# First three pairs' scores through four PSUM banks in place of two, with six entries of the emission table moved

## Chip, cores and metric

One NeuronCore of a Trainium2 chip runs the whole program. The metric is device microseconds (us) of one execution; the kernel before was timed three times, and a fourth execution was profiled.

## What is computed

Causal attention with a decay bias over 4 batches, 8 heads, 576 tokens and 64 channels a head; then a network with a spatial mix over the tokens, then one with a token shift. The numpy reference, cut:

```python
scores = (1/8) * q @ k.T
cum = cumsum(log(clip(f, 1e-4, 1)))
scores = where(causal, -1e9, scores + cum[:, None] - cum[None, :])
attn = exp(scores - max(scores)); attn = attn / (sum(attn) + 1e-9)
x = (attn @ v).transpose(0, 2, 1, 3).reshape(4, 576, 512)

h = relu(x @ w_in); u, v = h[..., :512], h[..., 512:]
x = (u * (w_spatial @ layernorm(v) + b_spatial)) @ w_out

xs = x shifted by one token
xk = mu_k * x + (1 - mu_k) * xs; xr = mu_r * x + (1 - mu_r) * xs
out = sigmoid(xr @ w_r) * (relu(xk @ w_k) ** 2 @ w_v)
```

## The kernel before

The 32 heads are worked in 16 pairs, p = 0 to 15, four to a batch. Most products keep fp32 accuracy by splitting an operand into two fp16 halves, high and low, and multiplying the halves.

A pair goes through these steps. Lines are in brackets.

- **Preparation.** ACT takes sums of squares of k and q (`qksq`, L70). PE totals them (L77), and DVE makes a power-of-two scale (L84, L85, L87, L243, L91). The high half of k is made on POOL (L254) from pair 1 on, that of q on DVE (L258); the low halves, nk and nq, on DVE (`qklo`, L266). SP then transposes each by DMA into kT and qT (L268). Copies of their halves go into kA (`kaux`, L274, L275) and qA (`qaux`, L280), with the decay rows.
- **Scores.** `score` (L298) writes, for each of two heads, four units u of one PSUM bank each: 512 columns; 448 and 64; 320 and 192; 64. Each column block is the sum of a kT by qT product and a kA by qA product. `rowmax` (L309, DVE) adds the mask, copies a unit into sx and keeps the row's maximum in nm. That frees the bank.
- **Row sums.** POOL makes nb from nm (L318), and ACT takes exponentials of sx with their sums (L321). `mrow` takes the logarithm on ACT (L330), splits the result into three halves on DVE (L331 to L335), transposes on PE (L337), copies to mr on DVE (L339) and sends three rows into qA by SP (L341).
- **Second scores.** `scoreT` (L352, PE) makes the transposed scores with those rows, ACT their exponentials e (L362, L358), POOL sets the causal zeros (L366, L360).
- **Products.** PE multiplies e by v (L393), ACT and DVE write the two halves of xt (L396, L400), and the first network starts on them: m1v (L530), m1u (L598), m2 (L615).

Beside the first pairs run the loads and the splitting of the first network's weight w_in, block by block: load into wst (L96), ACT L103, DVE L106, L110 and L111, ACT L70 for a sum of squares, then L446 on ACT and L447 on DVE.

PSUM is four pools of two banks: `psm` (tag m: an offset matmul at the start, then the first networks), `pss` (tag s: the scores), `pst` (tag t: second scores) and `pso` (products, totals and small transposes). The first networks also take banks of `pss` and `pst` later on.

The order comes from times. Each step is added with a planned time and a priority; the plan is run in order of time, and a scheduler that keeps the program's dependencies then sets each engine's order. Table P (L33) holds the offsets, in units of half a pair. `L1` to `L3` shift the whole preparation of pairs 1 to 3, by

```python
A = T - P[f"L{p}"]
```

so that a smaller entry makes it later. `wd` is the spacing of the w_in blocks, and `vl1`, `vl2` are the times at which v of batches 1 and 2 is loaded. In program text, tiles are rotated by three: qT_133, qA_134, kT_131 and kA_132 belong to pairs 1, 4, 7 and so on, qT_137, qA_138, kT_135 and kA_136 to pairs 2, 5, 8, and qT_129, qA_130, kT_127 and kA_128 to pairs 0, 3, 6. nm_159 serves even pairs, nm_160 odd ones.

Of the kernel before, what the change touches and what calls it, by code (L numbers as in the profile page):

```python
# [7 lines left out]
F32 = mybir.dt.float32  # L8
# [17 lines left out]
T3 = ((0, 0), (0, 1), (1, 0))  # L26
# [3 lines left out]
SU = (((4, 0, 512, 0),), ((3, 0, 448, 0), (4, 512, 64, 448)), ((2, 0, 320, 0), (1, 0, 192, 320)), ((0, 0, 64, 0),))  # L30


P = dict(load=-8.0, sq=-5.52, ss=-5.2, sc=-5.0, hik=-5.196, lok=-4.166, hiq=-4.2, loq=-3.95, aux=-3.539, s=-2.53, m=-0.78, t=0.0, tu=0.426, th=0.412, pv0=0.2, pv1=0.9, out=1.405, rc=1.219, nr=1.831, xs=0.977, xl=1.55, rs=0.06, w1=-3.8, w0=2.0, s1=1.5, s0=6.8, wd=0.6, sd=0.6, wsp=9.493, eb=13.318, ed=1.1, crow=-4.2, mlp0=2.7, mlp1=2.7, mlp2=3.608, mlp3=2.7, len0=6.684, len1=6.952, len2=6.757, len3=4.319, T1=0.0, T2=0.0, T3=0.02, T4=0.0, T5=0.0, T6=0.0, T7=0.044, L1=0.0, L2=-0.017, L3=0.0, L4=0.0, L5=-0.224, L6=-0.408, L7=0.04, v0=-3.174, vs0=0.15, T8=0.0, T9=0.0, T10=0.0, T11=0.0, T12=-0.061, T13=-0.031, T14=0.069, T15=0.0, L0=0.0, L8=0.0, L9=0.0, L10=0.0, L11=0.0, L12=0.0, L13=-0.003, L14=0.0, L15=-0.24, vl1=-5.062, vq1=-2.7, vl2=-4.971, vq2=-2.898, vl3=-3.679, vq3=-3.376, lv0=0.238, lu0=0.381, lg0=0.249, lv1=0.238, lu1=0.381, lg1=0.199, lv2=0.238, lu2=0.381, lg2=0.436, lv3=0.346, lu3=0.381, lg3=0.701, n1=0.385, n2=0.508, n3=1.019, n4=1.161, gs=0.05, ta=3.45, tb=1.65, tc=0.22, fnb=1, fnk=1, fvn=1, fwf=0, fwin=0, fwsp=0)  # L33

# [7 lines left out]
class K:  # L44
# [201 lines left out]
    def qkhi(self, p, nm, eng):  # L246
# [5 lines left out]
        if eng == "act":  # L252
            if P["fnk"] > 0.5 and p >= 1:
                self.nc.gpsimd.tensor_scalar(hi, src, s, None, op0=ALU.mult)  # L254
# [37 lines left out]
    def score(self, g, u):  # L292

        p, h = divmod(g, 2)
        s = self.s[u % 2] = self.pss.tile([128, 512], F32, tag="s", name="s")
        for ib, k0, n, o in SU[u]:
            for j, (qn, kn, r) in enumerate((("qT", "kT", 128), ("qA", "kA", 67))):
                self.nc.tensor.matmul(s[:, o:o + n], self.tok(qn, p, h, 128 * ib - 64, 128)[0:r], self.tok(kn, p, h, k0, n)[0:r], start=(j == 0), stop=(j == 1))  # L298
# [13 lines left out]
    def rowsum(self, g, blocks):  # L312
# [4 lines left out]
        nb = self.at.tile([128, 10], F32, tag="nb", bufs=4, name="nb")  # L317
        (self.nc.gpsimd if P["fnb"] > 0.5 else self.nc.vector).tensor_scalar(nb[:, c], self.nm[p % 2][:, c], qa[:, 5:6], -1.0, op0=ALU.mult, op1=ALU.mult)  # L318
        for ib in blocks:
# [107 lines left out]
    def wconv(self, i):  # L427
# [3 lines left out]
        wf = self.wf[i] = self.stp.tile([128, 512], F32, tag="wf", bufs=4, name="wf")  # L431
        self.raw_convert(self.wst[i], wf, True, P["fwf"] > 0.5)
        self.sumsq(self.am[:, kc:kc + 1], wf, self.win[:, 0, kc, cs])
# [6 lines left out]
    def wsplit(self, i):  # L440
# [4 lines left out]
        hi, lo = self.win[:, 0, kc, cs], self.win[:, 1, kc, cs]  # L445
        self.pin(nc.gpsimd.tensor_scalar(hi, wf, s, None, op0=ALU.mult) if P["fwin"] > 0.5 else nc.scalar.mul(hi, wf, s))  # L446
        nc.vector.scalar_tensor_tensor(lo, wf, s, hi, ALU.mult, ALU.subtract)  # L447

    def weights_spatial(self):
# [31 lines left out]
        for c in range(5):  # L481
            if c < 4:
                hi, lo, r = self.wspT[:, 2 + c], self.wspT[:, 6 + c], slice(0, 128)
            else:
                hi, lo, r = self.wspT[:, 0], self.wspT[64:128, 1], slice(64, 128)
            self.pin(nc.gpsimd.tensor_scalar(hi, ws[:, c], s, None, op0=ALU.mult) if P["fwsp"] > 0.5 else nc.scalar.mul(hi, ws[:, c], s))
            self.pin(nc.vector.scalar_tensor_tensor(lo, ws[r, c], s[r], hi[r], ALU.mult, ALU.subtract))
# [81 lines left out]
    def ln3(self, b, j):  # L569
        nc, tn = self.nc, KB[j][1]  # L570
        v, mv = self.vv[j]
        cp = nc.gpsimd.tensor_copy if P["fvn"] > 0.5 else nc.scalar.copy
        nc.vector.tensor_scalar(v[:tn], v[:tn], mv[:tn, 0:1], mv[:tn, 2:3], op0=ALU.subtract, op1=ALU.mult)
# [570 lines left out]
```

## Time and profile before

| | |
|---|---|
| three timed runs | 688.99, 689.62, 691.65 us; median 689.62 |
| profiled execution | 684.6 us, its span 682.9 us |
| PE busy | 616.9 us, 90% of the span |
| ACT busy | 462.7 us, 68% |
| DVE busy | 436.3 us, 64% |
| POOL busy | 186.5 us, 27% |
| mean granted TensorE clock | 0.98 |

The span runs from the first to the last instruction of the profiled execution. An engine's share is an average over stages that differ: the attention of the first pairs, before the networks have work for PE, is where PE's share is smallest. A wait in the trace names the engine that waits, what it waits for, and the engine that ended the wait.

### The profile page before, as it was taken

The page shows a single profiled execution, that of the slowest core. Times are in us where ns is not written, and L with a number is a line of the kernel's source. Part 1 is how long each engine was busy: PE and PEld are TensorE (multiplying, and loading weights), DVE is VectorE, ACT ScalarE, POOL GpSimd, SP SyncE. Part 2 cuts the span into 40 slices and gives each one's busy share as a digit, 9 for nine tenths or more (in the row PEclk, how much of TensorE's full clock was granted, in tenths as well). Part 3 has the DMA queues.
Part 4 walks back from the last instruction along what each step waited for, and adds up shares of the span by engine and source line. Part 5 has one row for each costly group of instructions (what it writes and reads, how often), then busy time and mean ns, then how long its engine had stood idle before and what let it go on. Part 6 is the DMA issues. An engine that isn't in the chain of part 4 may idle for free.

```text
span 682.9 us, 11117 instructions
## 1 busy us (share of the span) xinstructions
PE 616.9 (90%) x3720; PEld 369.7 (54%) x3720; DVE 436.3 (64%) x1238; ACT 462.7 (68%) x1023; POOL 186.5 (27%) x420
## 2 busy tenths in 40 slices
PE   0478676998999999989999899999999999999997
PEld 0133333566545666446657544566655556566585
DVE  6885957879487867676137888997228524532342
ACT  4689899898879879788339599974328334442531
POOL 6342444674447743465106010000000000000000
PEclk9998898999999999999999999999999999999999
DMA  7984542627654555341046672313001100100010
GB/s 254 266 229 94 139 116 52 207 57 196 167 129 108 94 172 132 74 91 33 19 154 212 206 253 70 123 62 108 15 1 32 62 1 0 62 1 0 1 62 31
DMA packets 69343, 69.74 MB, mean 102 GB/s; under 512 B 46659, under 2 KB 47395, under 8 KB 69286
## 3 DMA queue, kind: packets, MB, share of 16 engines
q1 hardware_dynamic: 68854, 67.85, 35.5%
q10 hardware_dynamic: 432, 1.18, 0.4%
q8 instruction: 29, 0.48, 0.3%
q14 instruction: 28, 0.23, 0.1%
HBM read 43.61 MB, written 9.55 MB: 78 GB/s over the span
## 4 chain that ended last, share of the span: by engine, by line
PE 59%; DVE 14%; DMA 10%; ACT 7%; SPq 3%; issue 3%; POOL 2%; DVEq 0%; ACTq 0%
PE m L927 37%; PE o L393 4%; PE t L352 4%; DVE sx L309 4%; PE m L615 4%; PE s L298 3%; PE m1u L598 3%; DMA qA<-qT 3%; PE m1v L530 3%; SPq L341 2%; DMA qT<-nq 2%; ACT junk L70 2%; DMA wst<-in_moe_w_r_dram 2%; ACT junka L321 1%; DMA kT<-nk 1%
## 5 line engine op out<-in xcount | busy, mean ns | idle before, releaser
L321 ACT ACTIVATE junka<-sx,nb,qa 128x576 bf16<-128x576 f32 (+4 forms) x160 | 103.8, 648 | 20.5 <-POOL nb L318 17.3
L927 PE MATMUL m<-moe_w_v,k 128*128 128x512 f32 x432 | 111.6, 406 | 0.0
L927 PE MATMUL m<-xx,moe_w_k 128*128 128x512 f16 (+1 forms) x480 | 99.1, 358 | 0.6 <-ACT tmp L976 0.6
L927 PEld LDWEIGHTS m<-moe_w_v,k 128*128 128x128 f32 x432 | 80.7, 188 | 19.4
L309 DVE CUSTOM_DVE_ANT_0 sx<-s,mask 128x512 f32<-128x512 f32 (+4 forms) x160 | 72.5, 473 | 21.5 <-PE s L298 17.6
L298 PE MATMUL s<-kT,qT 128*128 128x512 f16 (+2 forms) x192 | 55.3, 308 | 25.3 <-DVE nm L309 14.2
L362 ACT ACTIVATE e<-t,qa 128x512 f32<-128x512 f32 x96 | 64.1, 680 | 18.5 <-PE t L352 18.0
L366 POOL TENSOR_SCALAR_AFFINE_SELECT e<-e 128x128 f32<-128x128 f32 x128 | 48.1, 388 | 85.2 <-ACT e L362 82.5
L927 PEld LDWEIGHTS <-moe_w_k 128*128 128x128 f16 x480 | 45.5, 98 | 47.6 <-issue 5.3
L976 ACT ACTIVATE tmp<-m,sx 128x512 f32<-128x512 f32 (+1 forms) x40 | 25.9, 647 | 58.6 <-PE m L927 58.6
L977 DVE TENSOR_TENSOR tmp<-tmp 128x512 f32<-128x512 f32 (+1 forms) x40 | 25.5, 638 | 56.9 <-ACT tmp L976 56.9
L393 PE MATMUL o<-e,v 128*64 128x64 f32 (+4 forms) x384 | 55.0, 410 | 5.2 <-DVE mr L339 1.9
L298 PE MATMUL s<-kA,qA 67*128 67x512 f16 (+2 forms) x192 | 49.0, 307 | 9.1 <-DMA qA<-qT 5.8
L899 POOL COPY x<-x 128x1 f32<-128x1 f32 x16 | 4.8, 313 | 185.5 <-ACT x L897 175.7
L615 PE MATMUL m<-wspT,vn 128*128 128x288 f16 x384 | 55.2, 286 | 0.2
L927 PE MATMUL m<-gh,moe_w_out 128*128 128x512 f16 (+1 forms) x240 | 50.9, 367 | 3.3 <-DVE gs L803 3.3
L352 PE MATMUL t<-qA,kA 70*128 70x512 f16 (+2 forms) x192 | 48.9, 292 | 3.9 <-DMA qA<-mr 2.9
L598 PE MATMUL m1u<-xt,win 128*128 128x288 f16 x384 | 52.3, 287 | 0.0
L352 PE MATMUL t<-qT,kT 128*128 128x512 f16 (+2 forms) x192 | 50.8, 292 | 0.0
L530 PE MATMUL m1v<-win,xt 128*128 128x512 f16 x192 | 49.4, 392 | 0.6 <-ACT xt L396 0.6
L927 PE MATMUL m<-moe_w_r,xx 128*128 128x512 f16 x216 | 48.0, 379 | 0.0
L949 DVE SCALAR_TENSOR_TENSOR mt<-x,mu,mt 128x64 f32<-128x64 f32 (+4 forms) x64 | 30.2, 514 | 26.7 <-ACT mt L947 26.7
(219 smaller groups left out, 1134.7 us busy)
## 6 DMA issues: line engine op xcount, KB each, us to landing
knat<-in_k_dram SPq DMA_DIRECT2D x16, 320.0 KB
v<-in_v_dram SPq DMA_DIRECT2D x20, 256.0 KB
gd<-u SPq DMA_DIRECT2D x16, 288.0 KB
gl<-gd SPq DMA_DIRECT2D x8, 576.0 KB
out_dram<-o SPq DMA_DIRECT2D x18, 256.0 KB
qnat<-in_q_dram SPq DMA_DIRECT2D x14, 320.0 KB
wst<-in_moe_w_k_dram SPq DMA_DIRECT2D x8, 512.0 KB
g<-gd SPq DMA_DIRECT2D x16, 256.0 KB
```

The lines of the kernel that those rows point to most:

```text
L298: self.nc.tensor.matmul(s[:, o:o + n], self.tok(qn, p, h, 128 * ib - 64, 128)[0:r], self.tok(kn, p, h, k0, n)[0:r], start=(j == 0), stop=( ...
L309: self.nc.vector.tensor_tensor_reduce(out=self.sx[g][r0:, SO[ib] + k0:SO[ib] + k0 + n], in0=self.s[u % 2][r0:, o:o + n], in1=self.mask[r0: ...
L321: self.nc.scalar.activation(self.junka[r, 0:n], self.sx[g][r, SO[ib]:SO[ib] + n], AF.Exp, scale=qa[r, 5:6], bias=nb[r, i:i + 1], accum_out ...
L352: self.nc.tensor.matmul(t[:, o:o + n], self.tok(kn, p, h, 128 * c, 128)[0:r], self.tok(qn, p, h, q0, n)[0:r], start=(j == 0), stop=(j == 1))
L362: self.nc.scalar.activation(self.e[g][:, 512 * u:512 * u + 512], t, AF.Exp, scale=self.qa[p][:, 5:6])
L366: self.nc.gpsimd.affine_select(out=e, in_=e, pattern=[[1, 128]], compare_op=ALU.is_ge, fill=0.0, base=0, channel_multiplier=-1)
L393: self.chain(self.nc.tensor.matmul(o[r, 448 + f:448 + q1], v[:, c, pr, r], e, start=(c == 0), stop=(c == 4 or q1 == 64)))
L530: nc.tensor.matmul(self.m1p, xt[:, xs, 128 * j:128 * j + 128], self.win[:, ws, kc, 512:1024], **flags)
L598: self.nc.tensor.matmul(o, self.win[:, ws, kc, fs], self.xt[(4 * b + kc) % 8][:, xs, ts_], start=(kc == 0 and n == 0), stop=(kc == 3 and n ...
L615: nc.tensor.matmul(o, pairs[n][0], pairs[n][1], start=(n == 0), stop=(n == 13))
L927: self.nc.tensor.matmul(out, l, r, start=(first and j == 0), stop=(last and j == len(pairs) - 1))
L949: nc.vector.scalar_tensor_tensor(tmp[:, r0:r1], x2[:, kc, r0:r1], self.mu[:, w, 1, kc:kc + 1], tmp[:, r0:r1], ALU.mult, ALU.add)
```

## The change

Score units with an odd u of pairs 0, 1 and 2 take their bank from `psm` in place of `pss`. Six entries of the table move. No instruction is added or removed; the wait each score unit needs for its bank goes to another bank.

```diff
 P = dict(
...
-wd=0.6
+wd=0.664
...
-L1=0.0, L2=-0.017, L3=0.0
+L1=-0.036, L2=-0.11, L3=-0.093
...
-vl1=-5.062
+vl1=-5.303
...
-vl2=-4.971
+vl2=-4.818
...
     def score(self, g, u):

         p, h = divmod(g, 2)
-        s = self.s[u % 2] = self.pss.tile([128, 512], F32, tag="s", name="s")
+        s = self.s[u % 2] = self.psm.tile([128, 512], F32, tag="m", name="s") if p < 3 and u % 2 else self.pss.tile([128, 512], F32, tag="s", name="s")
```

The scheduler answers with other orders on all engines, up to the row of PE that stands about 205 us into the profile of before; behind it they are the same. Three places follow.

On DVE, where pair 0's rowmax begins (sx, nm_159) and a w_in block is converted (wst, wf), the difference reads:

```order
-L106 TENSOR_SCALAR wst<-wst 128x512
 L258 TENSOR_SCALAR nq<-qnat_89,qa 128x10x64
 L266 SCALAR_TENSOR_TENSOR nq<-qnat_89,qa,nq 128x10x64
+L266 SCALAR_TENSOR_TENSOR nk<-knat_86,qa,nk 128x10x64
+L309 ISA sx,nm_159<-s,mask 128x512
+L309 ISA nm_159 128x1
+L106 TENSOR_SCALAR wst<-wst 128x512
+L309 ISA sx,nm_159<-s,mask 128x448
```

Pair 1's nk and pair 0's first rowmax now stand ahead of that block's conversion, and the second unit is read while the block is still being converted.

On DVE, a little later, where pair 2 is prepared (qnat_90) and pair 1's rowmaxes run (nm_160), the rows of the change that are new or kept read:

```order
+L84 TENSOR_SCALAR qa<-o 128x2
+L85 TENSOR_SCALAR qa<-qa 128x2
+L309 ISA sx,nm_160<-s,mask 128x512
+L309 ISA nm_160 128x1
+L87 TENSOR_SCALAR qa<-qa 128x2
+L309 ISA sx,nm_160<-s,mask 128x448
+L309 ISA nm_160 128x1
+L309 ISA sx,nm_160<-s,mask,nm_160 128x64
+L309 ISA nm_160 128x1
 L243 SCALAR_TENSOR_TENSOR qa<-qa 128x1
 L258 TENSOR_SCALAR nq<-qnat_90,qa 128x10x64
```

Before, L84, L85 and L87 stood together with L243 and L258 behind them, and the rowmaxes of pair 1 came after nq; now the first three rowmaxes of head 0 come between L85 and L243.

On SP, from pair 2's first transpose on:

```order
 L268 DMA_TRANSPOSE qT_137<-nq 128x10x128
+L214 DMA qnat_90<-in_q_dram 128x640
+L268 DMA_TRANSPOSE kT_135<-nk 128x10x128
+L280 DMA qA_138<-qT_137 64x1280
+L341 DMA qA_130<-mr 1x10x128 x3
+L274 DMA kA_136<-kT_135 64x1280
+L214 DMA knat_87<-in_k_dram 128x640
+L214 DMA qnat_88<-in_q_dram 128x640
+L214 DMA knat_85<-in_k_dram 128x640
+L268 DMA_TRANSPOSE kT_127<-nk 128x10x128
+L341 DMA qA_134<-mr 1x10x128 x3
+L268 DMA_TRANSPOSE qT_129<-nq 128x10x128
```

Pair 2's copy into qA (qA_138) now stands ahead of pair 0's mr rows (qA_130); before it stood behind them. Pair 3's kT transpose (kT_127) stands ahead of pair 1's mr rows (qA_134), and its qT transpose behind them; before, both stood behind.

Further on, DVE's L331 to L335 of pair 2 come ahead of pair 3's first rowmax, where they came behind it and among the others.

## Rows read from the trace of the kernel before

**Rows 1.** Busy time by stretches: start:end, its length, busy time (instructions), clock, DMA share.

```profile
17.00:31.00 14.00, 7.06 (x26) 2.91 (x25) 12.36 (x35) 7.94 (x21) 5.02 (x6) 1.00 0.95 265
31.00:60.00 29.00, 20.83 (x106) 10.85 (x106) 21.55 (x88) 25.70 (x64) 12.03 (x21) 0.99 0.58 164
60.00:83.00 23.00, 16.09 (x79) 7.35 (x79) 18.49 (x56) 18.90 (x45) 8.70 (x15) 0.72 0.72 162
83.00:117.00 34.00, 24.40 (x172) 12.86 (x169) 22.64 (x94) 33.03 (x80) 15.45 (x30) 0.95 0.30 76
117.00:683.00 566.00, 546.86 (x3336) 334.13 (x3334) 349.90 (x942) 369.45 (x801) 133.93 (x308) 0.99 0.31 89
```

The columns after the length are PE, PEld, DVE, ACT and POOL.

**Rows 2.** Waits of 17 to 58 and 60 to 117: total, times, longest.

```profile
DVE sx L309 <- PE s L298: 2.5, 6, 0.6
...
PE s L298 <- DVE nm L309: 6.1, 6, 2.2
...
PE s L298 <- DVE nm L309: 6.4, 7, 2.8
```

**Rows 3.** Timeline of PE: scores of pairs 1 and 2, second scores of 2 and 4.

```profile
34.38 0.96 PE L298 MATMUL s<-kA,qA 67*128 67x512 f16 x2 [2.35 <-DMA qA<-qT]
...
47.07 0.59 PE L298 MATMUL s<-kA,qA 67*128 67x512 f16 x1 [0.42 <-DMA qA<-qT]
...
84.72 0.38 PE L352 MATMUL t<-qA,kA 70*128 70x512 f16 x1
...
116.33 0.59 PE L352 MATMUL t<-qA,kA 70*128 70x512 f16 x1 [1.40 <-DMA qA<-mr]
```

**Rows 4.** Timeline of DVE around pair 0's rowmax: start, duration, engine, line, tiles, idle.

```profile
20.56 1.76 DVE L111 SCALAR_TENSOR_TENSOR wf<-wst,wf 128x512 int32<-128x512 int32 x1
22.24 0.87 DVE L266 SCALAR_TENSOR_TENSOR nk<-knat,qa,nk 128x640 f16<-128x640 f32 x1
23.04 0.68 DVE L309 CUSTOM_DVE_ANT_0 sx<-s,mask 128x512 f32<-128x512 f32 x1
...
30.14 0.23 DVE L309 CUSTOM_DVE_ANT_0 sx<-s,mask 64x64 f32<-64x64 f32 x1
```

**Rows 5.** Timeline of SP's DMA queue, pairs 1 and 2.

```profile
25.49 1.77 SPq L268 DMA_TRANSPOSE qT<-nq  x1
...
30.06 0.47 SPq L280 DMA_DIRECT2D qA<-qT  x1
...
34.82 2.84 SPq L268 DMA_TRANSPOSE qT<-nq  x1
...
41.21 2.39 SPq L341 DMA_DIRECT2D qA<-mr  x3
...
44.34 0.54 SPq L280 DMA_DIRECT2D qA<-qT  x1
```

**Rows 6.** Timeline of DVE, preparation of pair 2.

```profile
32.08 0.16 DVE L84 TENSOR_SCALAR qa<-o 128x2 f32<-128x2 f32 x1 [1.70 <-PE o L77]
...
33.91 0.89 DVE L266 SCALAR_TENSOR_TENSOR nq<-qnat,qa,nq 128x640 f16<-128x640 f32 x1
```

**Rows 7.** The page's group of all rowmaxes: count, busy time, mean ns, idle.

```profile
L309 DVE CUSTOM_DVE_ANT_0 sx<-s,mask 128x512 f32<-128x512 f32 (+4 forms) x160 | 72.5, 473 | 21.5 <-PE s L298 17.6
```

**Rows 8.** Timeline of DVE, pair 2's mr.

```profile
72.08 1.29 DVE L331 SCALAR_TENSOR_TENSOR ln<-ln,qa,nm 128x10 f32<-128x10 f32 x1
...
80.59 0.28 DVE L339 CAST mr<-o 30x128 f16<-30x128 f32 x1
```

**Rows 9.** Timeline of ACT: pair 2's logarithm and pair 3's first exponential.

```profile
70.09 0.30 ACT L330 ACTIVATE ln<-sa,tiny 128x10 f32<-128x10 f32 x1
...
74.86 0.87 ACT L321 ACTIVATE junka<-sx,nb,qa 128x576 bf16<-128x576 f32 x1 [3.02 <-POOL nb L318]
```

**Rows 10.** Timeline of PE behind 117 us: the same product twice.

```profile
117.99 1.91 PE L530 MATMUL m1v<-win,xt 128*128 128x512 f16 x4
...
122.25 1.02 PE L530 MATMUL m1v<-win,xt 128*128 128x512 f16 x4
```

More of the change, by code (lines that the diff above doesn't have):

```diff
@@ L30 @@
 SU = (((4, 0, 512, 0),), ((3, 0, 448, 0), (4, 512, 64, 448)), ((2, 0, 320, 0), (1, 0, 192, 320)), ((0, 0, 64, 0),))
-P = dict(load=-8.0, sq=-5.52, ss=-5.2, sc=-5.0, hik=-5.196, lok=-4.166, hiq=-4.2, loq=-3.95, aux=-3.539, s=-2.53, m=-0.78, t=0.0, tu=0.426, th=0.412, pv0=0.2, pv1=0.9, out=1.405, rc=1.219, nr=1.831, xs=0.977, xl=1.55, rs=0.06, w1=-3.8, w0=2.0, s1=1.5, s0=6.8, wd=0.6, sd=0.6, wsp=9.493, eb=13.318, ed=1.1, crow=-4.2, mlp0=2.7, mlp1=2.7, mlp2=3.608, mlp3=2.7, len0=6.684, len1=6.952, len2=6.757, len3=4.319, T1=0.0, T2=0.0, T3=0.02, T4=0.0, T5=0.0, T6=0.0, T7=0.044, L1=0.0, L2=-0.017, L3=0.0, L4=0.0, L5=-0.224, L6=-0.408, L7=0.04, v0=-3.174, vs0=0.15, T8=0.0, T9=0.0, T10=0.0, T11=0.0, T12=-0.061, T13=-0.031, T14=0.069, T15=0.0, L0=0.0, L8=0.0, L9=0.0, L10=0.0, L11=0.0, L12=0.0, L13=-0.003, L14=0.0, L15=-0.24, vl1=-5.062, vq1=-2.7, vl2=-4.971, vq2=-2.898, vl3=-3.679, vq3=-3.376, lv0=0.238, lu0=0.381, lg0=0.249, lv1=0.238, lu1=0.381, lg1=0.199, lv2=0.238, lu2=0.381, lg2=0.436, lv3=0.346, lu3=0.381, lg3=0.701, n1=0.385, n2=0.508, n3=1.019, n4=1.161, gs=0.05, ta=3.45, tb=1.65, tc=0.22, fnb=1, fnk=1, fvn=1, fwf=0, fwin=0, fwsp=0)
+P = dict(load=-8.0, sq=-5.52, ss=-5.2, sc=-5.0, hik=-5.196, lok=-4.166, hiq=-4.2, loq=-3.95, aux=-3.539, s=-2.53, m=-0.78, t=0.0, tu=0.426, th=0.412, pv0=0.2, pv1=0.9, out=1.405, rc=1.219, nr=1.831, xs=0.977, xl=1.55, rs=0.06, w1=-3.8, w0=2.0, s1=1.5, s0=6.8, wd=0.664, sd=0.6, wsp=9.493, eb=13.318, ed=1.1, crow=-4.2, mlp0=2.7, mlp1=2.7, mlp2=3.608, mlp3=2.7, len0=6.684, len1=6.952, len2=6.757, len3=4.319, T1=0.0, T2=0.0, T3=0.02, T4=0.0, T5=0.0, T6=0.0, T7=0.044, L1=-0.036, L2=-0.11, L3=-0.093, L4=0.0, L5=-0.224, L6=-0.408, L7=0.04, v0=-3.174, vs0=0.15, T8=0.0, T9=0.0, T10=0.0, T11=0.0, T12=-0.061, T13=-0.031, T14=0.069, T15=0.0, L0=0.0, L8=0.0, L9=0.0, L10=0.0, L11=0.0, L12=0.0, L13=-0.003, L14=0.0, L15=-0.24, vl1=-5.303, vq1=-2.7, vl2=-4.818, vq2=-2.898, vl3=-3.679, vq3=-3.376, lv0=0.238, lu0=0.381, lg0=0.249, lv1=0.238, lu1=0.381, lg1=0.199, lv2=0.238, lu2=0.381, lg2=0.436, lv3=0.346, lu3=0.381, lg3=0.701, n1=0.385, n2=0.508, n3=1.019, n4=1.161, gs=0.05, ta=3.45, tb=1.65, tc=0.22, fnb=1, fnk=1, fvn=1, fwf=0, fwin=0, fwsp=0)
 PRIO = 300
```

## The prediction

> **What bounds the kernel now.** I read the busy time by stretches first, then the waits, then the timelines around the first pairs. In the table by stretches [rows 1] look at PE against the length of each stretch: from 117 us to the end it works 546.86 of 566 us, so what is early or late there stays so to the end. Before 117 PE idles (6.9 of 14, 8.2 of 29, 6.9 of 23, 9.6 of 34 us) and another engine sets the pace: DVE in 17 to 31 (12.36 of 14, with the DMA engines at 0.95), ACT in 31 to 60 (25.70 of 29) and again in 83 to 117 (33.03 of 34). Between these ACT stretches, in 60 to 83, ACT has 4.1 us free. So a change among the first pairs is worth what it does to ACT's clock position at 83 and to PE's at 117, and no more.
>
> The waits [rows 2] show what four banks aim at: PE waits 6.1 us in 17 to 58 for a rowmax to free a bank, and 6.4 us in 60 to 117. Two readings limit this. The second sum belongs to pairs 3 to 5, whose scores keep two banks. And in 17 to 58 DVE, the other side of the exchange, waits only 2.5 us for PE: the rowmaxes, not the matmuls, are the longer half.
>
> **The banks.** Eight score units of each of the first three pairs now turn through four banks. PE writes all four before the first is free, so the most this can give is DVE's wait, 2.5 us over three pairs [rows 2], and the least is nothing. Pair 2's share of it (about half) falls after 47 us, where ACT is full, so I take 1.2 us, and only on DVE. The lenders lose nothing: the first networks' first matmul comes after these scores, since it needs pair 0's xt.
>
> The Trainium skill (Perfetto Trace Analysis, Matmuls) says that independent matmul groups should turn through different banks, so that the evacuation of one lies under the next one's matmuls; by that rule the 6.1 us of PE's wait would go. The rows on DVE disagree with taking that sum whole; what it would give is the second case below. Against the change speaks another page of the Trainium skill (TensorE: Matmul & The Clock Gate, A second HAM failure mode: psum-queue depth-cycling): cycling through banks left PE idle between groups often enough for its clock to go up and down. Here the 512-column matmul of pair 2's scores took 0.59 us at 47.07, and one at 84.72 took 0.38 [rows 3]; the scores of the first pairs run at the lower of the two rates already (though the column of the granted clock says 0.99 there [rows 1]), so no rate is there to be lost. By that page the sum would be worse only if the stretch behind them, 60 to 83 at a mean of 0.72, grew longer.
>
> **Pair 0's rowmax and the w_in block.** Ahead of pair 0's first rowmax stand L110, L111 (1.76 us, slowed) and pair 1's nk (0.87) [rows 4]. L106, L110 and L111 of that block now go behind nk and the first rowmax. So it starts up to 1.76 us earlier than 23.04; I take 1.6, 21.4, since its own scores bound it too. The last rowmax ends now at 30.37; with less waiting for PE inside and one conversion less, I take 1.2 to 1.8 us earlier. ACT takes these rows as they come but then waits for pair 1 anyway: gain on the path nothing, cost of the delayed block nothing (the first network that uses it waits for pair 0's xt, far behind). If that cover is gone, it costs L111's time, 1.76.
>
> **Pair 1's preparation.** nk is produced about 1.8 us earlier, and its two transposes are issued back to back, with knat behind them. qT goes out at 25.49 and its copy to qA at 30.06 [rows 5]; the scores that need it start at 34.38, after 2.35 us of waiting for that DMA [rows 3]. I take 1.7 to 2.4 us earlier, 32.0 to 32.7. Bounds: nothing, since the DMA engines are busy at 0.95 there and an earlier issue may only queue longer, and 2.4.
>
> **Pair 2's preparation, the added wait.** Before, L84 to the nq of L266 ran ahead of pair 1's rowmaxes (32.08 to 34.80 [rows 6]). Now L87, L258 and L266 stand behind rowmaxes that need pair 1's scores. These can't start before about 33.0 (32.0 to 32.7 and a matmul). Head 0's five rowmaxes take 2.4 us at a mean of 473 ns [rows 7]; the preparation takes 2.72 us from 32.08 to 34.80, of which the first short ones are done by then, so 2.0 to 2.6. nq ends at 37.4 to 38.0, 2.6 to 3.2 us late. Its cover is SP's queue: qT is issued at 34.82 but its qA copy (L280) only at 44.34, because kT's transpose and pair 0's three mr rows (41.21, 2.39) stand ahead [rows 5]. Now L280 stands ahead of L341. So pair 2's scores, at 47.07 [rows 3], move by 0 to +1 us, and pair 0's mr rows by +1 to +1.5. Both fall where ACT has exponentials waiting, so I cost them at nothing; without that cover they would cost that 1 us.
>
> **Pair 2's mr rows, the main term.** On ACT the logarithm L330 of pair 2 moves ahead of several of pair 1's exponentials, and on DVE L331 to L335 move ahead of pair 3's rowmax. Before, L331 at 72.08 was followed by L339 only at 80.59 [rows 8], since rowmaxes and weight splitting lay between, and scoreT of pair 2 ran at 84.72 [rows 3]. L330 would come at about 67 instead of 70.09 [rows 9]; some 5 us of DVE's work stand between it and L339 in the new order, so L339 at about 72.7; with the 4.1 us that now lie between L339 and scoreT, scoreT at about 76.8: 8 us earlier. The price is on pair 3: its first rowmax waits behind L258, L266 and L447, +0.9 to +2 us. What this does to ACT decides. ACT idles 3.02 us before 74.86 because POOL's nb is late [rows 9]. POOL's queue ahead of that nb ends 1.3 to 2.3 us sooner when pair 1's exponentials do, and pair 2's exponentials then fill later gaps. So ACT is 1.3 to 2.3 us ahead at about 75 and, being full from 83 on, carries this to 117. There scoreT of pair 4 starts at 116.33 after 1.40 us for its own mr DMA [rows 3]; its chain (L330, DVE, SP) moves with ACT. Here I take 2.0 us from ACT and 0.5 us from pair 5's transposes, now issued ahead in SP's queue.
>
> **Sum:** banks 0 on the path, pair 0 and pair 1 covered, pair 2's late nq 0, mr rows -2.0, SP's queue -0.5: -2.5 us. The profiled execution took 684.6 us (span 682.9); it stands 5.0 us under the median of the three runs, 689.62. I move the median by the sum: **687.1 us** (the profiled execution would be 682.1).
>
> **The clock as an unknown.** From 116.33 the 512-column matmuls run at half rate: four m1v products take 1.91 us at 117.99 and 1.02 at 122.25 [rows 10]. Where that stretch falls depends on idle time before it, which this change moves. One block of four costs or saves 0.9 us; I take nothing and keep ±0.9.
>
> **Rivals.**
> A, the forecast, -0.5 to -4.5 us, chance 0.40; a quarter of it lies beyond 0.5% (3.45 us, about what a measurement here can tell from no change).
> B, the gaps really close: ACT's free 4.1 us in 60 to 83 and 1.0 us in 83 to 117 are all filled, 5.1 us, and with them scoreT's 1.40 us and one half-rate block of 0.9, up to 7.4: 683.6 at -6. For it: pair 2's scoreT and pair 1's last products move by 8 us or more, far more than ACT's idle time. Against: four banks touch only 2.5 us of DVE's waiting. That the 6.1 us of bank waits vanish, whole, would give the same -6. Chance 0.27.
> C, slower: pair 1's transposes land no earlier, because the DMA queues are full at 0.95 [rows 1]. Then its qA still comes at 34.4, pair 2's nq, queued behind its rowmaxes, ends at 39.5 to 40 instead of 34.80, its L280 at 46 to 47 instead of 44.34, and its scores start 2.5 to 3 us late; ACT, at 25.70 of 29, loses that and gets the L341 delay on top, up to 5 us. It decides from pair 1's scores later than about 33.0. Price +2.5 to +5, 693.1 at +3.5. Chance 0.23, of it 0.19 beyond 0.5%.
> D, nothing: the new order only reshuffles work under ACT and DVE, and the gain before 75 us is eaten by pair 3's later rowmax; within ±1 us, 689.6. Chance 0.10.
>
> **The numbers.** Likeliest A: 687.1. Faster by over 0.5%: 0.10 of A and B, 0.37. Within: 0.30 of A, 0.04 of C, D: 0.44. Slower: 0.19. The range for 8 in 10 takes in B nearly to its end (681.5) and C to +3.9 (693.5); outside are the ends of both.
>
> **What would show it.** Right: pair 0's first rowmax near 21.4, pair 1's qA scores near 32, pair 2's scores between 47 and 48, its scoreT near 76.8, ACT's gap before pair 3's exponentials under 2 us, scoreT of pair 4 near 114, PE's waits after that as now. Wrong: pair 1's scores still near 34.4 (C), or pair 3's rowmax later than 71 with ACT's gap still 3 us (D), or ACT without a gap from 60 to 117 and scoreT of pair 4 before 112 (B). PE's wait for banks in 17 to 58 should fall below 2 us in every case; if that alone happens and the time stands, the wait was never on the path. If 60 to 83 shows a lower clock than 0.72, the clock took part of the gain.

## The result, and the profile after

The changed kernel takes 695.13 us (median of six runs, 694.23 to 697.32) against 689.99 us for the kernel before (six runs, 688.83 to 691.65). The ratio is 1.0082 with a 95% interval of 1.0053 to 1.0110: slower by 5.1 us. The prediction, 687.1, had the wrong sign; the time lies outside its range of 681.5 to 693.5 and on the side of rival C.

The profiled execution of the change took 697.32 us, 2.2 over its median, where that of before, at 684.6 us, stood 5.4 under the 689.99. So about 7.6 of the 12.7 us between the two spans (682.9 and 695.6) belong to the executions that happened to be profiled. This is kept in mind in all that follows: medians decide, marks show where.

The table by stretches of the changed kernel, beside [rows 1] (start:end, length, then PE, PEld, DVE, ACT, POOL, granted clock, DMA share, GB/s):

```profile
17.00:31.00 14.00, 7.05 (x28) 3.11 (x27) 11.18 (x35) 7.12 (x19) 5.30 (x6) 1.00 1.03 260
31.00:60.00 29.00, 20.23 (x85) 9.74 (x83) 20.16 (x82) 24.80 (x61) 10.34 (x19) 1.00 0.61 166
60.00:83.00 23.00, 16.57 (x109) 8.15 (x106) 16.91 (x49) 18.37 (x41) 11.17 (x16) 0.93 0.72 166
83.00:117.00 34.00, 26.95 (x133) 13.57 (x133) 19.01 (x83) 28.98 (x70) 10.70 (x25) 0.70 0.32 70
117.00:683.00 566.00, 544.07 (x3333) 332.46 (x3333) 354.18 (x963) 376.61 (x818) 138.45 (x314) 0.98 0.31 89
```

In 83 to 117 ACT works 28.98 us where it worked 33.03, and there the granted clock has its low part (0.70, before 0.95), which lay in 60 to 83 before (0.72, now 0.93). The 4.1 us that ACT had free in 60 to 83 are not filled: now they are 4.6, and in 83 to 117 ACT has 5.0 us free in place of 1.0. A second profile of the kernel before, shown below, has 3.3 us free there, so part of that last difference is chance.

Its waits in 17 to 58, beside [rows 2] (total, times, longest):

```profile
PE s L298 <- DMA kT<-nk: 8.7, 2, 7.4
...
PE s L298 <- DMA qT<-nq: 4.1, 1, 4.1
...
DVE sx L309 <- PE s L298: 1.4, 2, 1.2
...
PE s L298 <- DVE nm L309: 0.6, 1, 0.6
```

The wait for banks has gone from 6.1 to 0.6 us. A wait of 4.1 us for pair 1's transposed q stands in its place.

PE's timeline, beside [rows 3] and [rows 10]:

```profile
33.22 0.96 PE L298 MATMUL s<-kA,qA 67*128 67x512 f16 x2 [0.99 <-DMA qA<-qT]
...
47.32 0.61 PE L352 MATMUL t<-qA,kA 70*128 70x512 f16 x1
...
49.00 1.00 PE L298 MATMUL s<-kA,qA 67*128 67x512 f16 x2
...
65.42 0.38 PE L352 MATMUL t<-qA,kA 70*128 70x512 f16 x1 [2.36 <-DMA qA<-mr]
...
80.61 1.04 PE L530 MATMUL m1v<-win,xt 128*128 128x512 f16 x4 [1.05 <-ACT xt L396]
81.93 0.38 PE L352 MATMUL t<-qA,kA 70*128 70x512 f16 x1
...
106.89 1.87 PE L530 MATMUL m1v<-win,xt 128*128 128x512 f16 x4
...
125.43 0.59 PE L352 MATMUL t<-qA,kA 70*128 70x512 f16 x1 [1.21 <-DMA qA<-mr]
```

Pair 1's scores come 1.2 us earlier than before (34.38), pair 2's 1.9 later (47.07), pair 2's second scores 2.8 earlier (84.72), pair 4's second scores 9.1 later (116.33). Most of what parts the two profiles stands there already, though the second profile of the kernel before shows that some 5 us at that place are chance.

DVE's timeline, beside [rows 4, 6, 8]: pair 0's first and last rowmax, pair 2's nq, pair 3's first rowmax, pair 2's mr.

```profile
21.13 0.69 DVE L309 CUSTOM_DVE_ANT_0 sx<-s,mask 128x512 f32<-128x512 f32 x1 [0.20 <-PE s L298]
...
27.85 0.23 DVE L309 CUSTOM_DVE_ANT_0 sx<-s,mask 64x64 f32<-64x64 f32 x1
...
37.03 1.91 DVE L266 SCALAR_TENSOR_TENSOR nq<-qnat,qa,nq 128x640 f16<-128x640 f32 x1
...
72.41 0.68 DVE L309 CUSTOM_DVE_ANT_0 sx<-s,mask 128x512 f32<-128x512 f32 x1
...
76.10 0.27 DVE L339 CAST mr<-o 30x128 f16<-30x128 f32 x1
```

SP's queue, beside [rows 5]: pair 1's qT and qA, pair 2's qT and qA, pair 0's mr rows.

```profile
23.80 3.11 SPq L268 DMA_TRANSPOSE qT<-nq  x1
...
29.83 0.47 SPq L280 DMA_DIRECT2D qA<-qT  x1
...
38.97 1.80 SPq L268 DMA_TRANSPOSE qT<-nq  x1
...
42.99 0.66 SPq L280 DMA_DIRECT2D qA<-qT  x1
43.84 2.38 SPq L341 DMA_DIRECT2D qA<-mr  x3
```

ACT's timeline, beside [rows 9]: pair 2's logarithm, pair 3's first exponential, pair 3's logarithm.

```profile
68.79 0.29 ACT L330 ACTIVATE ln<-sa,tiny 128x10 f32<-128x10 f32 x1
...
78.42 0.87 ACT L321 ACTIVATE junka<-sx,nb,qa 128x576 bf16<-128x576 f32 x1 [3.39 <-POOL nb L318]
...
95.44 0.30 ACT L330 ACTIVATE ln<-sa,tiny 128x10 f32<-128x10 f32 x1
```

The gap before 78.42 has not shrunk (3.39, before 3.02). The page's group of rowmaxes [rows 7] keeps its mean:

```profile
L309 DVE CUSTOM_DVE_ANT_0 sx<-s,mask 128x512 f32<-128x512 f32 (+4 forms) x160 | 72.5, 473 | 20.5 <-PE s L298 18.7
```

At this point rival C looked shown: pair 1's copy into qA went out at 29.83 (30.06 before), its scores came at 33.22, later than the 33.0 from which C was to decide, and pair 2's nq ended 4.1 us later. The experiments went after that first, and it turned out not to carry the larger part of the loss. The sign set for rival D came as well: pair 3's first rowmax at 72.41, later than 71, with ACT's gap still over 3 us.

### The profile page after: what moved, and what is told of

Same layout as the page of the kernel before. It is cut to its first block, busy times and chain, and to the rows that moved or that the text cites. A ratio compares the mean times of both kernels' runs of the same rounds, so it can differ in the third digit from the quotient of the medians.

```text
span 695.6 us, 11115 instructions
## 1 busy us (share of the span) xinstructions
PE 625.1 (90%) x3720; PEld 373.3 (54%) x3720; DVE 435.0 (63%) x1238; ACT 465.4 (67%) x1023; POOL 187.3 (27%) x420
## 4 chain that ended last, share of the span: by engine, by line
PE 56%; ACT 12%; DVE 12%; DMA 11%; issue 3%; POOL 3%; SPq 3%; DVEq 0%; ACTq 0%; POOLq 0%
PE m L927 37%; PE t L352 4%; PE m L615 4%; DMA kT<-nk 3%; PE o L393 3%; DVE sx L309 3%; PE s L298 3%; ACT junka L321 2%; PE m1v L530 2%; DMA qA<-qT 2%; PE m1u L598 2%; ACT junk L70 2%; SPq L341 2%; DMA wst<-in_moe_w_k_dram 1%; DMA wst<-in_moe_w_r_dram 1%
## 5 line engine op out<-in xcount | busy, mean ns | idle before, releaser
L298 PE MATMUL s<-kT,qT 128*128 128x64 f16 (+2 forms) x192 | 54.7, 313 | 17.8 <-DMA kT<-nk 10.4
L366 POOL TENSOR_SCALAR_AFFINE_SELECT e<-e 128x128 f32<-128x128 f32 x128 | 44.9, 364 | 88.0 <-ACT e L362 87.3
L393 PE MATMUL o<-e,v 128*64 128x64 f32 (+4 forms) x384 | 58.5, 431 | 7.8 <-DVE mr L339 4.8
L298 PE MATMUL s<-kA,qA 67*128 67x192 f16 (+2 forms) x192 | 48.3, 312 | 7.7 <-DMA qA<-qT 5.2
L530 PE MATMUL m1v<-win,xt 128*128 128x512 f16 x192 | 50.8, 402 | 1.4 <-ACT xt L396 1.4
```

The source lines that it names most:

```text
L366: self.nc.gpsimd.affine_select(out=e, in_=e, pattern=[[1, 128]], compare_op=ALU.is_ge, fill=0.0, base=0, channel_multiplier=-1)
L393: self.chain(self.nc.tensor.matmul(o[r, 448 + f:448 + q1], v[:, c, pr, r], e, start=(c == 0), stop=(c == 4 or q1 == 64)))
L530: nc.tensor.matmul(self.m1p, xt[:, xs, 128 * j:128 * j + 128], self.win[:, ws, kc, 512:1024], **flags)
```

## Experiments

Ratios are against runs of the kernel before on the same chip, with 95% intervals.

### The kernel before, once more

No edit; one more execution, profiled.

> The kernel before, unchanged, for a second trace of it: its first profiled execution took 684.6 us, 5 us under the median of its timed runs. If that execution was a lucky one, this one shows 688 to 691 us, and somewhere a stretch of low clock or a longer wait that the first did not have; the pair-by-pair starts of the mr rows (41.2, 56.3, 80.9, 95.6, 112.8 us for pairs 0 to 4) show where.

Measured: 694.65 us, span 692.9, mean clock 0.972 (0.98 in the first profile). With the same instructions in the same order, pair 4's mr rows went out at 117.7 instead of 112.8. So a mark of one profile carries some 5 us of chance at 115 us, and only differences that many kernels share, or medians, can be read. Its row for 83 to 117:

```profile
83.00:117.00 34.00, 28.27 (x166) 14.63 (x165) 20.39 (x89) 30.72 (x75) 11.05 (x28) 0.82 0.28 73
```

ACT works 30.72 of 34 us here, where [rows 1] had 33.03: how full ACT is in that stretch differs between two executions of one kernel.

### Banks without the table, the table without banks

The first has four banks and the table of before, the second adds the three `L` entries, the third has the whole new table and two banks.

```diff
# e1
+        s = self.s[u % 2] = self.psm.tile([128, 512], F32, tag="m", name="s") if p < 3 and u % 2 else self.pss.tile([128, 512], F32, tag="s", name="s")
# e2: as e1, and
+L1=-0.036, L2=-0.11, L3=-0.093
# e3: two banks, and
+wd=0.664, L1=-0.036, L2=-0.11, L3=-0.093, vl1=-5.303, vl2=-4.818
```

> Four banks alone, the table of before. Theory Q (queues): with four banks the scheduler puts pair 2's nq behind rowmaxes of pair 1 and lets pair 2's scores run ahead of pair 0's second scores on PE, so pair 1's mr rows go out at about 61 to 62 us instead of 56.3 and this delay is carried to the end: 693 to 696 us. Theory K (clock): the loss comes after 75 us, where PE runs dry after pair 2's products were moved forward and then works at half rate; here pair 2's mr rows stay late, as before, so 688 to 691 us. Theory T (table): only the shifted table costs: 688 to 691 us as well, but then e3 is slow.

> Four banks and the three preparation shifts (L1 to L3), without the change of wd, vl1 and vl2. Its order is near that of the change up to pair 4. Q: as e1, 693 to 696 us. K: pair 2's mr rows come early (about 76 us), so PE runs dry near 75 to 90 us and works at half rate after it: 693 to 696 us while e1 is near 690. T: near 695.

> The shifted table with two banks throughout. Its order differs from the others far into the program, so its total also carries that. Q: pair 1's mr rows go out at about 56 to 57 us, as before, and the time up to pair 4 is that of before: 688 to 692 us. K: as pair 2's mr rows fall, early and slow or late and not. T: 694 to 697 us.

Measured: 694.81 (1.0069, 1.0039 to 1.0099), 694.24 (1.0077, 1.0044 to 1.0111) and 706.86 (1.0236, 1.0187 to 1.0285). Four banks with the old table already lose what the change loses; the new table without them loses far more than any expectation had. In the first, pair 1's mr rows went out at 59.14, earlier than theory Q had them (61 to 62), at the time that Q expected. But the scheduler orders anew for every edit of banks or table, so each of the three is also another order.

### Which pair's banks, and TensorE's rate

Four banks for pairs 0 and 1 alone, for pairs 0 and 2 with the old table, for pair 0 alone; then the change with twelve unused 512-column matmuls between pair 1's last score and pair 0's transposes, so that TensorE does not rest there.

```diff
# e4
-... if p < 3 and u % 2 else ...
+... if p < 2 and u % 2 else ...
# e5, table of before
+... if p in (0, 2) and u % 2 else ...
# e6
+... if p == 0 and u % 2 else ...
# e7: change, and
+def warm(k, g, n, w=None):
+    for i in range(n): w = w or k.psm.tile([128, 512], F32, tag="m", name="warm"); k.nc.tensor.matmul(w, k.ident, k.tok("kT", 1, 1, 0, 512), start=True, stop=True)
...
-            add(T + P["m"], 0, self.mrow, p)
+            add(T + P["m"], 0, self.mrow, p); [add(T + P["s"] -0.050, 4, warm, self, 2, 12) for p2 in (2,) if p == 2]
```

> The change with pair 2 back on two banks (p < 2 for p < 3). SP's order stays that of the change throughout, and DVE's rejoins it before row 145; what differs is that on PE pair 2's scores no longer run ahead of pair 0's second scores. Theory P (PE's order): in 44 to 60 us PE is full at half rate, and four banks for pair 2 put its scores in front of pair 0's second scores and of the transpose that pair 1's mr rows wait for. Then here the mr rows of pair 1 go out at 58.5 to 60 us instead of 62.0 and the time is 690 to 693 us. Theory D (DVE's order): the loss comes from pair 2's nq behind pair 1's rowmaxes, which stays: mr rows of pair 1 at 61 to 62, 694 to 696 us.

> Four banks for pairs 0 and 2 only, with the table of before (e1 with pair 1 on two banks). DVE does pair 2's nq behind three of pair 1's rowmaxes and not behind all of head 0's. Theory D: nq ends about 1 us earlier than in e1 and pair 0's mr rows with it (43.5 in e1 to 42 to 43), and the time falls from e1's 694.8 to 691 to 693 us. Theory P: pair 2 still runs ahead on PE, 694 to 695 us.

> The change with four banks for pair 0 alone. Theory P: as e4 or better, 690 to 692 us. Theory D: pair 2's nq still stands behind rowmaxes of pair 1, so 693 to 696 us. If the loss were in the order after 60 us, which here is that of neither kernel, the time can fall outside both.

> The change with 12 added matmuls of 512 columns, results unused, between pair 1's last score and the transpose of pair 0's mr rows, where PE waited 5.4 us for DVE (12 of them at half rate are 5.1 us). Nothing is left out. Theory K (rate): if the half rate of 44 to 58 us is what makes the added PE work cost, PE now comes out of its idle time working and its rate rises sooner: pair 0's second scores at 47 us take 0.38 us for 512 columns instead of 0.63, pair 1's mr rows go out at 57 to 60 us instead of 62.0, and the time falls to 690 to 693 us. If the rate is not the cause: rows at 62, 694 to 697 us.

Measured: 694.52 (1.0083, 1.0048 to 1.0118), 696.16 (1.0097, 1.0062 to 1.0132), 696.46 (1.0106, 1.0070 to 1.0141), 695.23 (1.0091, 1.0061 to 1.0121). With the new table, four banks in pair 0 alone are enough for a loss of that size, and that pair 2's scores are ordered otherwise on PE is not needed for it. In the last one, pair 0's second scores ran at 0.38 us a matmul (0.61 in the change), but the added matmuls also held pair 0's mr rows back to 47.9; it says that the rate there is not the whole cause, no more.

### Other tables, near the orders of before and of the change

Only the table moves here, and in the third the banks too, so as to get an early or a late nq of pair 2, and SP's two exchanges, with two and with four banks.

```diff
# e8, two banks: nq early, on SP pair 3's kT ahead of pair 1's mr rows
+L1=-0.059, L2=-0.15, L3=-0.126, vl1=-5.2
# e9, two banks: nq late, SP as in the change
+L1=-0.012, L2=-0.324, L3=-0.094, vl1=-5.303
# e10, four banks: nq early, SP as in the change
+L1=0.007, L2=0.487, L3=0.014, vl1=-5.2
# e11, two banks: nq early, SP as in the change
+L1=-0.002, L2=0.457, L3=-0.032, vl1=-5.2
```

> Two banks as before, four table entries (L1 -0.059, L2 -0.15, L3 -0.126, vl1 -5.2). DVE keeps the order of before (pair 2's nq ahead of pair 1's rowmaxes, pair 0's mr rows ahead of pair 2's copy into qA); on SP only pair 3's kT transpose goes ahead of pair 1's mr rows. Theory order (the late nq of pair 2 and, behind it, SP's queue): pair 2's nq ends near 35, pair 0's mr rows go out near 41.3, pair 1's at 58.5 to 60.5, since they now wait for the transpose that waits for pair 0's second scores; 690 to 693 us. If the SP order of pair 1's mr rows alone carries the loss: 694 to 696. If the banks carry it: 690.

> The order of the change with two banks throughout: pair 2's nq behind six rowmaxes of pair 1, on SP pair 2's copy into qA ahead of pair 0's mr rows, pair 3's kT ahead of pair 1's mr rows (L1 -0.012, L2 -0.324, L3 -0.094, vl1 -5.303). Theory order: nq ends at 37 or later, pair 0's mr rows near 44, pair 1's at 60 to 62, and 694 to 697 us, as in the change. Theory banks (the exchange of banks itself costs): the same marks may move, but the time is 690 to 691.

> Four banks for pairs 0 to 2, with a table (L1 0.007, L2 0.487, L3 0.014, vl1 -5.2) that keeps pair 2's nq ahead of all of pair 1's rowmaxes on DVE; on SP pair 2's copy into qA and some loads still stand ahead of pair 0's mr rows, and pair 3's kT ahead of pair 1's. Theory order, if the late nq is what costs: nq ends near 35, pair 0's mr rows 41.5 to 43, second scores of pair 0 near 45, 689 to 692 us. Theory banks, or if the order on SP alone costs: 694 to 696.

> Two banks; pair 2's nq ahead of pair 1's rowmaxes on DVE as before, but on SP the order of the change: pair 2's copy into qA and loads ahead of pair 0's mr rows, pair 3's kT ahead of pair 1's mr rows (L2 0.457, L1 -0.002, L3 -0.032, vl1 -5.2). If the late nq costs: nq near 35, 689 to 692 us. If SP's order costs by itself: pair 0's mr rows 43 to 44, pair 1's 59 to 61, 694 to 696. If the banks cost: 690.

Measured: 692.47 (1.0055, 1.0021 to 1.0088), 692.12 (1.0049, 1.0013 to 1.0084), 696.30 (1.0099, 1.0068 to 1.0129), 691.83 (1.0040, 1.0004 to 1.0077). Pair 2's nq on DVE, first of the kernel with two banks and a late nq, then of the one with four banks and an early one:

```profile
38.19 0.87 DVE L266 SCALAR_TENSOR_TENSOR nq<-qnat,qa,nq 128x640 f16<-128x640 f32 x1
```

```profile
32.93 0.89 DVE L266 SCALAR_TENSOR_TENSOR nq<-qnat,qa,nq 128x640 f16<-128x640 f32 x1
```

The late one costs 0.5%, the early one 1.0%. So the time does not follow pair 2's nq, and the theory that I had drawn from the first profile, that the late nq carries the loss, falls. The three kernels with two banks are shorter than this one with four, and than the four-bank ones above, which would speak against the banks themselves; but their orders differ too, up to some 200 us. Their mean clock is higher as well, 0.9744 to 0.9757 against 0.9710; over all runs of the kernel before, 0.01 of it goes with 5.3 us, so that 1.8 to 2.5 of the 3.8 to 4.5 us between the medians go with the clock (an estimate).

### The order held

To part the banks from the order, four kernels add nothing but dependencies without a wait: each instruction of an engine is tied behind the one that is to stand ahead of it. `ORDER` lists each engine's instructions by their number in the program.

```diff
-        body(tc, args, out)
+        body(tc, args, out); fix_order(tc)
...
+def fix_order(tc):
...
+    ins = list(tc.nc.cur_bb.bb.instructions)
+    for part in zlib.decompress(base64.b64decode(ORDER)).decode().split("|"):
+        at, prev = 0, None
+        for d in part.split(":")[1].split(","):
+            at += int(d)
+            if prev is not None:
+                tc.add_manual_dep(ins[at], prev.name, mybir.DependencyInfo(mybir.DependencyClass.NoSync, mybir.DependencyReason.DATA))
+            prev = ins[at]
```

> Four banks for pairs 0 to 2, with every engine (PE, DVE, ACT, POOL, SP) held to the order of before by extra dependencies without a wait: only the banks differ. If the loss comes from the order that the four banks let the scheduler choose: 689.5 to 691.5 us, as before, with PE's wait for banks still shorter than 6.1 us. If the banks cost by themselves (scores that run earlier, rate or contention): 693.5 to 696.

Measured: 689.77 us (686.61 to 694.81), ratio 0.9990, 0.9961 to 1.0020. In its trace every engine has the order of before. So in that order four banks by themselves cost nothing and give nothing that this interval shows (2.7 us down, 1.4 up). Its waits in 17 to 58:

```profile
PE s L298 <- DMA kT<-nk: 8.2, 2, 7.4
...
PE s L298 <- DMA qT<-nq: 4.2, 1, 4.2
...
PE s L298 <- DVE nm L309: 1.2, 1, 1.2
DVE sx L309 <- PE s L298: 1.2, 3, 0.6
```

PE's 6.1 us for banks are down to 1.2, and PE now waits 4.2 us for pair 1's transposed q (none before) and 0.8 us more for kT: it has written what it can and waits for the next pair. DVE's wait for PE is 1.2 us in place of 2.5.

> Four banks, DVE, ACT, POOL and SP held to the order of before, PE held to the order of the kernel with four banks and the old table (measured at 694.81): kT products of several units ahead of their qA products, second scores and scores of pair 2 in the new order. If PE's order costs: 693.5 to 696. If DVE's and SP's order cost: 689.5 to 691.5.

> Two banks; DVE, ACT, POOL and SP held to the order of the kernel with four banks and the old table (694.81), PE free to follow with two banks. If the order on these engines (pair 2's nq behind pair 1's rowmaxes, pair 0's mr rows behind pair 2's copy into qA) costs: 693.5 to 697, with pair 0's mr rows at 43.5 or later. If PE's order or the banks cost: 689.5 to 691.5.

> The changed table with two banks throughout; DVE, ACT, POOL and SP held to the very order of the change, PE free to follow with two banks. If the order on these engines carries the loss of the change (695.13): 694 to 697. If the four banks or PE's order carry it: 690 to 692.

Measured: 714.47 (1.0365, 1.0337 to 1.0394), 707.40 (1.0253, 1.0216 to 1.0289), 700.10 (1.0147, 1.0118 to 1.0176). An order on PE taken from one kernel and an order on the other engines from another lose more than either kernel: this tells nothing of PE's order alone, since no kernel has it. The last one took longer than either of its expectations had, and says something of the change: with its own order on DVE, ACT, POOL and SP, two banks take 700.10 and four take 695.13, where PE's order was free to follow the banks and differs too. In 17 to 58 PE waits 7.2 us for banks with two and 0.6 with four. So within that order the banks, together with the order that PE takes under them, are worth 0.6% (1.0147 against 1.0082), some 4.5 us; in the order of before they are worth nothing that shows.

### The order of before to 58 us, then that of the change, and the reverse

Four banks and a held order in both. The point of exchange is the step at which pair 1's mr rows go out. A helper that keeps certain steps in program order is switched off, since the held order sets them.

```diff
     def pin(self, ins):
...
-        self.tc.keep_in_program_order(ins)
+        return ins
```

> Four banks for pairs 0 to 2; every engine held to the order of before up to the step at which pair 1's mr rows go out (about 58 us), and to the order of the change behind it. If the early order costs (pair 2's nq behind pair 1's rowmaxes, and with it pair 0's chain from the logarithm to the mr rows and SP's queue): 688 to 691.5 us, pair 0's mr rows at 41 to 42.5, pair 1's at 56 to 58.5. If the late order costs (pair 2's logarithm ahead of pair 1's exponentials, pair 3's rowmaxes behind pair 2's mr rows): 694 to 697.

Measured: 694.94 us (691.97 to 699.55), ratio 1.0073, 1.0041 to 1.0106.

> Four banks for pairs 0 to 2; every engine held to the order of the change up to the step at which pair 1's mr rows go out (about 60 us), and to the order of before behind it: the mirror of the run before this one. If only the late order costs (pair 2's second scores and their exponentials among pair 3's, shown by the run before at 694.94): 689 to 691.5 us. If the early order (late nq of pair 2, pair 0's and pair 1's mr rows 1.5 to 4 us late) costs by itself as well: 693 to 696, and the two costs don't add up, since both together give 695.13.

Measured: 692.22 us (687.52 to 693.92) against 690.97 in its own group, ratio 1.0009, 0.9975 to 1.0043. It lies between the two ranges expected. So the larger part of the loss by the medians lies in the order behind 58 us. The early order costs 3.0 us at most by its interval, but that it costs nothing is not shown: pair 2's mr rows go out 1.7 us later with it (84.46 against 82.75 of the kernel with banks and the order of before), pair 9's 1.8 us later (222.67 against 220.83). Its runs also had a higher mean clock than those of before in the same group (0.9758, 0.9739), those of the late order a lower one (0.9714, 0.9751). At 5.3 us for 0.01 this is 1.0 us hidden in the one and 2.0 us added in the other; set to the same clock, the early order would stand some 2 us above before and the late one some 3 (an estimate).

What the late order does is read from SP's mr rows of pairs 2, 3 and 4, first with four banks and the order of before throughout:

```profile
82.75 2.34 SPq L341 DMA_DIRECT2D qA<-mr  x3
...
97.48 2.29 SPq L341 DMA_DIRECT2D qA<-mr  x3
...
117.24 2.31 SPq L341 DMA_DIRECT2D qA<-mr  x3
```

then with the order of the change behind 58 us:

```profile
74.17 2.33 SPq L341 DMA_DIRECT2D qA<-mr  x3
...
100.24 2.35 SPq L341 DMA_DIRECT2D qA<-mr  x3
...
118.62 2.31 SPq L341 DMA_DIRECT2D qA<-mr  x3
```

Pair 2 is 8.6 us earlier, pair 3 is 2.8 later, pair 4 is 1.4 later. ACT shows the exchange. Order of before: pair 2's logarithm, the first exponentials of pair 3's first and second head, pair 3's logarithm, the last exponential of pair 2's second scores.

```profile
71.79 0.31 ACT L330 ACTIVATE ln<-sa,tiny 128x10 f32<-128x10 f32 x1
...
76.70 0.87 ACT L321 ACTIVATE junka<-sx,nb,qa 128x576 bf16<-128x576 f32 x1 [3.17 <-POOL nb L318]
...
84.11 0.85 ACT L321 ACTIVATE junka<-sx,nb,qa 128x576 bf16<-128x576 f32 x1
...
90.80 0.30 ACT L330 ACTIVATE ln<-sa,tiny 128x10 f32<-128x10 f32 x1
...
96.92 0.37 ACT L358 ACTIVATE e<-t,qa 128x128 f32<-128x128 f32 x1
```

Order of the change behind 58 us, the same five; pair 2's last exponential now stands third:

```profile
66.63 0.29 ACT L330 ACTIVATE ln<-sa,tiny 128x10 f32<-128x10 f32 x1
...
75.85 0.87 ACT L321 ACTIVATE junka<-sx,nb,qa 128x576 bf16<-128x576 f32 x1 [3.09 <-POOL nb L318]
...
88.35 0.37 ACT L358 ACTIVATE e<-t,qa 128x128 f32<-128x128 f32 x1 [0.66 <-PE t L352]
88.62 0.86 ACT L321 ACTIVATE junka<-sx,nb,qa 128x576 bf16<-128x576 f32 x1
...
93.89 0.30 ACT L330 ACTIVATE ln<-sa,tiny 128x10 f32<-128x10 f32 x1
```

Pair 2's second exponentials end 8.6 us earlier, because they run among pair 3's first head; pair 3's second head starts 4.5 us later, and its logarithm comes 3.1 later. In these two traces ACT has done the same work in another order, and the pair that later pairs queue behind is the late one. In the profiles, 1.2 us of it are left at pair 9 (mr rows at 222.06 against 220.83), and 4.8 at the end of the span (692.9 against 688.1). Between them, at 240 to 260, lies a stretch with a lower clock in the second of these two kernels, and not in the first. The first row is that of the order of before, the second that of the order of the change behind 58 us:

```profile
240.00:260.00 20.00, 19.75 (x164) 13.65 (x163) 12.93 (x46) 16.16 (x37) 10.02 (x22) 1.00 0.67 160
```

```profile
240.00:260.00 20.00, 17.97 (x132) 11.97 (x132) 11.16 (x39) 13.02 (x32) 9.30 (x19) 0.91 0.66 162
```

That stretch does not go with the late order: the changed kernel, which has that order, reads 1.00 there (first row), and the first of the tables tried above, with two banks and pair 3's logarithm early at 88.4, reads 0.91 (second row).

```profile
240.00:260.00 20.00, 17.75 (x146) 11.94 (x145) 14.42 (x48) 14.97 (x39) 12.76 (x21) 1.00 0.69 149
```

```profile
240.00:260.00 20.00, 18.31 (x140) 12.58 (x140) 11.88 (x41) 13.15 (x33) 9.97 (x21) 0.91 0.65 157
```

Over their twelve runs each, the mean clock is 0.9746 and 0.9714. Over 120 runs of the kernel before, a run with 0.01 less is 5.3 us longer, so that 0.0032 stand for some 1.7 of the 5.2 us between the medians (an estimate). By the marks the exchange on ACT stands for 1.2 us (pair 9) to 2.8 (pair 3), but the early order, which the medians hardly show, stands for 1.8 at pair 9: marks of that size decide nothing. What is left over, and whether the late order lowers the mean clock of its runs, no run here settles.

Open, too: the kernel with four banks and the old table (694.81), the one with four banks for pairs 0 and 2 (696.16) and the one with the early nq (696.30) lose about as much, though in them pair 3's logarithm comes at 90.58, 91.49 and 90.01, about as with the order of before (90.80). The kernel with two banks and the late nq has pair 2's mr rows early (76.21) and pair 3's logarithm late (92.78), and loses less (692.12). So the exchange on ACT is neither needed for such a loss nor shown to be what makes it in the change; that it is remains an argument from two traces.

No kernel of this study is shorter than the one before by more than the intervals.

## Why the prediction was wrong, by its own steps

**The banks: 0 on the path, 1.2 us on DVE.** Right for the order of before, and shown by holding it: PE's bank wait falls from 6.1 to 1.2 us, DVE's from 2.5 to 1.2, the time stands (0.9990). The rule of the Trainium skill that was weighed (Perfetto Trace Analysis, Matmuls: independent groups through different banks) would have promised those 6.1 us. The wait does go, as the rule has it; the time does not follow there, since PE then waits for the transposes. In the order of the change the banks, together with PE's order, were worth some 4.5 us, which the forecast did not have.

**Pair 0's rowmax at 21.4.** Right: 21.13, the last one 2.3 us earlier (1.2 to 1.8 forecast). What it is worth was not measured by itself.

**Pair 1's scores at 32.0 to 32.7.** Wrong: 33.22. Pair 1's qT is issued 1.69 us earlier (25.49 to 23.80) but occupies 3.11 us in place of 1.77, beside DMA engines at 1.03 in place of 0.95. So its copy into qA went out only 0.23 us earlier, near the bound "nothing, since an earlier issue may only queue longer"; the scores came 1.2 us earlier, between that bound and the 1.7 to 2.4 taken.

**"Pair 2's late nq 0."** The size was off, and whether the cost was nothing is open. Its nq ends at 38.94, where 37.4 to 38.0 stood, because L266 took 1.91 us in place of 0.89; pair 2's scores came 1.9 us later, pair 0's mr rows 2.6 (0 to 1 and 1 to 1.5 forecast). Yet the order that does this, by itself, gives 1.0009, 3.0 us at most by its interval and some 2 us at the same clock (an estimate). Rival C had named this place, its trigger came true, and the sum lies on its side; but its price, +2.5 to +5 us, is for the most part not there. That the sum lies where C put it is for the larger part luck.

**"Mr rows -2.0."** This is the step that failed. The early marks came as forecast in kind: pair 2's logarithm, L339 and second scores all moved forward (68.79, 76.10, 81.93; 67, 72.7 and 76.8 forecast). But the order behind 58 us, of which this step is the part that the forecast priced, gives 1.0073 by itself, some 5 us, on the other side (some 3 at the same clock). The working had ACT 1.3 to 2.3 us ahead at about 75 and, "being full from 83 on", carrying this to 117. With the late order alone ACT is 0.85 us ahead at pair 3's first exponential (75.85 against 76.70), and 4.5 us behind at that of the second head (88.62 against 84.11): the lead is not carried, since pair 2's second exponentials run in between. Nor was ACT as full as one profile had it: 33.03 of 34 us there, 30.72 in the second. The working asked what earlier mr rows release and answered with idle time of ACT. It did not ask in whose place their exponentials run. The price that it did put, +0.9 to +2 us on pair 3's first rowmax, was at the wrong place: with the late order alone that rowmax comes at 70.25, against 70.73 with the order of before. The gap before pair 3's first exponential, which the forecast meant to fill, is as long as before (3.39, and 3.09 with the late order alone, against 3.02), since POOL's nb ends it either way. How much of the loss behind 58 us is this exchange, and how much the rest of that order or the clock, stays open.

**"SP's queue -0.5."** No mark bears it out: with ACT's gain it was to bring scoreT of pair 4 to about 114, which came at 125.43, its wait for its own mr rows 1.21 in place of 1.40.

**The clock.** The forecast said that a lower clock in 60 to 83 would take part of the gain. That stretch has a higher one (0.93), and 83 to 117 the lower (0.70). This does go with the late order: by itself it has 0.93 and 0.75, where four banks in the order of before have 0.69 and 0.86.

**The median.** Taking the sum from the median and not from the profiled execution was right: the profile of before was among the shortest of all runs.

## What to carry to other kernels

Where an engine is full for a stretch, a step that is moved forward on it can move others back (here one went 8.6 us forward and another 4.5 back): before counting what the early one gains, name the one whose place it takes, and who waits for that. A change of buffers under a scheduler is two changes, the buffers and the order; holding the order by dependencies without a wait parts them, and here it put the loss on the order. To call a part of the order the cause, it too has to be run alone, at a clock that can be compared. A rival whose first marks all come true is still not shown until its part is run alone.

## What the runs showed of the hardware that was not expected

The same kernel, in the same order, took 684.58 to 697.24 us over 120 runs, and the time goes with the mean granted clock (correlation -0.72, 5.3 us for 0.01). A single profile of it can therefore stand 5 us from the median, as the first one did.

The column of the granted clock and the matmuls differ early: in 31 to 60 the changed kernel's row says 1.00, yet its 512-column matmul takes 0.61 us at 47.32, and 0.38 at 65.42 where it runs at the higher rate. The rate there is better read from the duration of a shape that recurs.

One conversion, L266 on 128x640, takes 0.87 to 0.89 us in most places, and 1.91 at 37.03 in the changed kernel. It takes 1.91 to 1.93 there in six other kernels with much the same order on DVE too, and in all seven POOL's L284 (1.33 us) has begun 0.1 us before it; in the kernel before L266 begins first, and takes 0.89. That POOL is what slows it was not tried.
